# Value products two score tiles at a time at the end, a second buffer for the last normalizations, the last products in halves, and z parts marked by landing time

## The chip, the cores and the metric

The kernel runs on one core of one Trainium2 chip. The metric is device time in microseconds for one execution of the program.

## What is computed

One fused block: a layernorm, then multi-head attention and a gated MLP side by side on the same normalized input, added to the input.

```python
B, S, D, H = 1, 2048, 512, 32                 # 16 elements a head
xn = layernorm(x)
# A: attention
q, k, v = split(xn @ wqkv)                    # 32 heads
o = softmax(q @ k.T / 4) @ v
A = concat_heads(o) @ wo
# B: gated MLP, 1792 features, halves of 896
z  = gelu(xn @ w_in)
z1, z2 = z[..., :896], layernorm(z[..., 896:])
g  = einsum("ts,bsf->btf", w_sp, z2) + b_sp   # mixes the 2048 rows
Bo = (z1 * g) @ w_out
return x + A + Bo
```

All of it is float32. Most products are made of three products of high and low parts.

## The kernel before

**Attention sets the beat.** Heads go in 16 pairs `p`, queries in 4 blocks `c` of 512, keys in 16 blocks of 128, so there are N = 1024 score tiles (`order`, numbered `n`; a tile is 128 keys by 512 queries for the two heads). A tile passes three steps. `scores()` multiplies (TensorE, L1149) into one of three PSUM buffers `sl[0..2]`; `exp` turns it into a tile `pf` (ScalarE, L76; 8 buffers); `values()` multiplies a phase of CYC = 8 such tiles with V (TensorE, L1246), two tiles at a time in four column strips, summing in one `sl` buffer. Here a phase is named by its first tile: V984 takes tiles 984 to 991. The sum of the first phase of a block is copied by ScalarE, that of the second is added by VectorE (`part_out`, L1266).

**The maxima.** The softmax's maximum comes from a second pass over scores with queries on the partitions: `maxima()` (TensorE, L1163), reduced by VectorE (L868), one tile each. For 16 of them `max_fin` writes rows that go through DRAM into `qst`, as rows of the score product. The maxima run some tiles ahead of the scores and end first (n_mx == NSTEP).

**All other products** are cut into "dense slots" of two matmuls into the two banks of `dps` (L1208): Q, K, V, the MLP's two inputs, the spatial mix (`spatial`, on tiles `wsp` and parts `zs` of z2 loaded by `load_z`), the MLP's output and the attention's output (`attn_out`, 18 slots for every two row blocks). Where nothing else can go, a filler multiplies zeros (L1222).

**The order** is written out by a planner at build time: its loop takes, from the strings ORDER, one of S (score tile), M (maximum tile), D (dense slot) or V (value phase) and keeps due times `T` of each engine. What the plan says is fixed; on the chip every instruction waits on semaphores. When a generator of dense slots says "w" (`need`), the planner plans other things until the condition holds.

**The end.** The heads of group 3 (p = 12 to 14) are normalized in `norm_out`, for each `c`: loads of the sums (`os`) and of the unnormalized outputs (`ob`), a reciprocal, a trip through DRAM, products on GpSimd (L911 to L931), giving `ohl`, which `attn_out` needs for the row blocks of that `c`. One buffer `os` and one `ob` serve them all (`room["ogrp"]`). The last pair, p = 15, skips DRAM: `last_pair` (L992) spreads sums with a selector matrix, `last_norm` divides (VectorE, L998 and L1000), `last_mm` multiplies by the last rows of wo (L1007; four matmuls into two `sl` buffers), `last_add` adds to `fin` (VectorE, L1014), and SyncE stores the rows. `last_turn` decides when `last_mm` goes.

Of the kernel before, what the change touches and what calls it, by code (L numbers as in the profile page):

```python
# [47 lines left out]
CYC = 8  # L48
LOAD = 5.0
HALF = 2.7  # L50
# [8 lines left out]
def fused_block(ctx, tc, x, wqkv, wo, w_in, w_spT, b_sp, w_out, out):  # L59
# [614 lines left out]
    zp, z1s = {}, {}  # L674
# [31 lines left out]
    def spatial():  # L706
        for n, (g, (x, y)) in enumerate(units):
# [184 lines left out]
    def norm_out(g4, c):  # L892
# [31 lines left out]
        lease("ogrp", 1)  # L924
# [71 lines left out]
    def last_norm(c, acc, rec, on, k):  # L996
# [5 lines left out]
        turn.append((c, on, ends[0] + 0.1))  # L1002

    def last_mm(c, on, ks):
        for a in range(4):
            u = slice(32 * a, 32 * a + 32)
            nc.tensor.matmul(sl[ks[a // 2]][:, a % 2, :], on[u, :], sel["ones"][u, 1, :], start=True, stop=True)  # L1007
        T["P"] += 0.9
        for i, k in enumerate(ks):
            spawn(last_add(4 * c + 2 * i, k), 0, T["P"] + 0.2)  # L1010
# [23 lines left out]
    with tc.manual_schedule(engines=engines):  # L1034
# [139 lines left out]
        def has_dense(t):  # L1174
            nonlocal blocked, swap, hold, seen
            while not slots:
# [11 lines left out]
                elif it[0] == "q":  # L1188
                    hold = spent > 11 and n_pv < N
# [42 lines left out]
        def values():  # L1232
# [3 lines left out]
            window[:] = T["P"], T["P"] + CYC / 2 * ROUND  # L1236
            k = take("o")
            for n in range(n_pv, n_pv + CYC, 2):
# [3 lines left out]
                for r in range(2):  # L1242
                    pf = full.pop(n + r)
                    for j in range(2):
                        cols = VW * (2 * j + r)
                        nc.tensor.matmul(sl[k][cols:cols + VW, 0, :], vpack(kt + r, 2 * p + j), pf[:, j * 512:(j + 1) * 512], start=n == n_pv, stop=n == n_pv + CYC - 2)  # L1246
# [3 lines left out]
            n_pv += CYC  # L1250
            spawn(part_out(p, c, kt0 == 0, k), 0, T["P"] + 0.22)
# [27 lines left out]
        def last_turn(t):  # L1279
            c, on, when = turn[0]  # L1280
            if when > t or any(added.get(4 * c + 2 * i, FAR) + 0.1 > t for i in range(2)):
                return False
            if len(spare(t)) < 2:
                return False
            turn_to("L")
            ks = [take("l"), take("l")]
            last_mm(c, on, ks)
# [3 lines left out]
        while n_pv < N or queue or tasks or late or urgent or turn or slots:  # L1291
# [4 lines left out]
            if turn and (n_st - n_pv < 2 or n_pv == N) and last_turn(t):  # L1296
# [6 lines left out]
            gone = {"S": n_st == N, "M": n_mx == NSTEP, "D": ahead > 0 or not has_dense(t), "V": n_pv == N}[op]  # L1303
# [53 lines left out]
```

## Time and profile before

| | us |
|---|---|
| median of 3 runs (lowest, highest) | 1860.66 (1859.05, 1863.14) |
| the profiled execution: its own time | 1862.6 |
| the profiled execution: span of its instructions | 1860.4 |
| TensorE busy (share of the span) | 1811.4 (97%) |
| VectorE busy | 1441.5 (77%) |
| ScalarE busy | 1189.1 (64%) |
| GpSimd busy | 722.3 (39%) |
| the same, from 1765 to 1860 only: TensorE, VectorE, ScalarE | 84.8, 51.2, 49.7 of 95 |

A row of the timeline reads: start, length, engine, line, operation, output<-inputs, shapes, count, and in brackets the idle time before it and what ended that. A matmul's length includes its pipeline, so the distance between two starts is what a matmul costs. PE is TensorE, DVE VectorE, ACT ScalarE, POOL GpSimd, SP SyncE.

### The profile page before, as it was taken

To read this page: it belongs to the slowest core of one execution; us is meant where nothing else is said; L and a number is where in the kernel's file an instruction comes from. 1 tells how busy PE (TensorE), PEld (TensorE's weight loads), DVE (VectorE), ACT (ScalarE), POOL (GpSimd) and SP (SyncE) were. 2 spreads that over 40 slices of the span, in tenths; PEclk is the share of its full clock that TensorE was granted. 3 is DMA by queue.
4 is the path that set the end of the run, shared out by engine and by line. 5 is a ranking of instruction groups with operands and counts; after the bars stand their busy time and mean duration, and the time that the engine had idled before them with its cause. 6 is when DMAs were issued, how large, how long until landed. Compare 5 with 4: busy or idle time off the path is not lost.

```text
span 1860.4 us, 38081 instructions
## 1 busy us (share of the span) xinstructions
PE 1811.4 (97%) x14804; PEld 1099.5 (59%) x14804; DVE 1441.5 (77%) x1677; ACT 1189.1 (64%) x1292; POOL 722.3 (39%) x808
## 2 busy tenths in 40 slices
PE   6999999999999999999999999999999999999998
PEld 4766566655655565556565665656556566656544
DVE  6578778888887787878877787778778887887873
ACT  2157777687777777666666665666666665666655
POOL 5324342778888767222442245103422230001110
PEclk9999999999999999999999999999999999999999
DMA  6728772533565346656857558565767676575322
GB/s 227 283 98 282 277 242 87 127 92 110 136 215 134 106 113 204 156 156 162 217 166 199 157 179 206 158 150 155 193 168 182 174 185 143 129 182 149 112 78 90
DMA packets 212124, 306.14 MB, mean 165 GB/s; under 512 B 36816, under 2 KB 108048, under 8 KB 209056
## 3 DMA queue, kind: packets, MB, share of 16 engines
q1 hardware_dynamic: 202824, 273.83, 53.5%
q0 software_dynamic: 9120, 29.89, 4.8%
q8 instruction: 116, 1.90, 0.4%
q14 instruction: 64, 0.52, 0.1%
HBM read 193.80 MB, written 109.85 MB: 163 GB/s over the span
## 4 chain that ended last, share of the span: by engine, by line
PE 84%; DVE 6%; DMA 4%; POOL 3%; issue 2%; ACT 1%; SPq 1%; DVEq 0%; POOLq 0%; ACTq 0%
PE dps L1208 34%; PE sl L1246 23%; PE sl L1149 13%; PE sl L1163 12%; DVE mm L868 4%; PE dps L1222 1%; DMA zs<-z2scr 1%; DMA kscr<-qkhl 1%; SPq L132 1%; ACT pf L76 1%; POOL wsp L291 1%; DMA wsp_15r<-in_w_spT 0%; POOL wsp L289 0%; DMA wsp_0r<-in_w_spT 0%; DMA qst<-mscr 0%
## 5 line engine op out<-in xcount | busy, mean ns | idle before, releaser
L868 DVE TENSOR_REDUCE mm<-sl 128x2 f32<-128x1024 f32 x1024 | 1224.4, 1222 | 203.7 <-PE sl L1163 199.1
L76 ACT ACTIVATE pf<-sl 128x1024 f32<-128x1024 f32 x1024 | 1041.1, 1026 | 338.8 <-PE sl L1149 297.3
L1246 PE MATMUL sl<-pf,vall 128*32 128x512 f32 x4096 | 468.4, 598 | 0.7 <-DVE mm L868 0.4
L1149 PE MATMUL sl<-qst,kst 50*128 50x512 f32 x2048 | 437.8, 419 | 11.1 <-DVE mm L868 4.3
L1163 PE MATMUL sl<-kst,qst 48*128 48x512 f32 x2048 | 424.0, 406 | 4.5 <-DVE mm L868 2.2
L1208 PE MATMUL dps<-wsp,zs 64*128 64x512 f32 x2352 | 382.1, 393 | 2.6 <-DMA zs<-z2scr 2.6
L1149 PEld LDWEIGHTS sl<-qst,kst 50*128 50x128 f32 x2048 | 195.8, 184 | 218.4 <-issue 79.3
L1246 PEld LDWEIGHTS sl<-pf,vall 128*32 128x32 f32 x4096 | 120.5, 110 | 271.2 <-issue 237.4
L1163 PEld LDWEIGHTS sl<-kst,qst 48*128 48x128 f32 x2048 | 196.5, 185 | 105.9 <-ACT pf L76 55.3
L1208 PEld LDWEIGHTS dps<-wsp,zs 64*128 64x128 f32 x2352 | 229.3, 187 | 40.4 <-DMA zs<-z2scr 4.1
L76 ACT ACTIVATE e<-sl 128x512 f32<-128x512 f32 x64 | 38.3, 598 | 208.0 <-PE sl L1246 198.0
L1266 DVE TENSOR_TENSOR e<-sl,e 128x512 f32<-128x512 f32 x64 | 44.3, 692 | 136.4 <-PE sl L1246 70.2
L774 POOL TENSOR_TENSOR hhl<-z1i,hhl 128x512 fp32r<-128x512 f32 x28 | 35.9, 1292 | 275.8 <-ACT hhl L76 275.8
L1208 PE MATMUL dps<-w,xt 64*128 64x448 f32 x768 | 110.6, 368 | 1.5
L1208 PE MATMUL dps<-wout,hp 64*128 64x512 f32 x672 | 110.3, 392 | 0.0
L915 POOL TENSOR_TENSOR ob<-ob 128x512 f32<-128x512 f32 (+1 forms) x16 | 20.5, 1284 | 201.5 <-DMA ob<-rscr 186.6
L1208 PEld LDWEIGHTS dps<-w,xt 64*128 64x128 f32 x768 | 73.9, 186 | 16.0 <-issue 7.8
L1208 PEld LDWEIGHTS dps<-wout,hp 64*128 64x128 f32 x672 | 65.5, 187 | 9.1
L911 POOL TENSOR_TENSOR ob<-ob 128x512 f32<-128x512 f32 (+1 forms) x16 | 21.0, 1315 | 117.5 <-DMA ob<-escr 117.5
L441 POOL TENSOR_TENSOR qkhl<-qr,qkhl 128x512 fp32r<-128x512 f32 x24 | 30.4, 1286 | 69.9 <-ACT qkhl L76 65.8
L1208 PE MATMUL dps<-wf,zs 64*128 64x512 f32 x336 | 55.5, 392 | 0.1
L1208 PE MATMUL dps<-xnT,wqk 64*128 64x512 f32 x288 | 47.7, 395 | 1.1 <-ACT vall L76 0.4
(289 smaller groups left out, 1691.0 us busy)
## 6 DMA issues: line engine op xcount, KB each, us to landing
zs<-z2scr SPq DMA_DIRECT2D x192, 256.0 KB
escr<-e SPq DMA_DIRECT2D x60, 256.0 KB
hscr<-hhl POOLq DMA_DIRECT2D x28, 512.0 KB, 6.6
qst<-qscr SPq DMA_DIRECT2D x30, 384.0 KB
kst<-kscr SPq DMA_DIRECT2D x30, 384.0 KB
qscr<-qkhl SPq DMA_DIRECT2D x16, 512.0 KB
kscr<-qkhl SPq DMA_DIRECT2D x16, 512.0 KB
xscr<-xnT POOLq DMA_DIRECT2D x16, 512.0 KB, 5.0
```

The source lines that it names most:

```text
L76: return nc.scalar.activation(out, in_, func, **kw)
L132: nc.sync.dma_start(raw(dst), raw(src))
L441: nc.gpsimd.tensor_sub(hl[:, 1, :], raw_, hl[:, 0, :].bitcast(F32))
L774: nc.gpsimd.tensor_sub(hl[:, 1, :], z1, hl[:, 0, :].bitcast(F32))
L868: nc.vector.tensor_reduce(mmax[g][:, :, t, kc], sl[k], AX.X, ALU.max)
L911: nc.gpsimd.tensor_add(both_[rows, 0, :], both_[rows, 0, :], both_[rows, 1, :])
L915: nc.gpsimd.tensor_mul(both_[rows, 0, :], both_[rows, 0, :], both_[rows, 1, :])
L1149: nc.tensor.matmul(sl[k][:, j, :], kst[p % 2][rows, kt * P:(kt + 1) * P], qst[p % 2][rows, c * 512:(c + 1) * 512], start=True, stop=True)
L1163: nc.tensor.matmul(sl[k][:, j, :], qst[p % 2][rows, tt * P:(tt + 1) * P], kst[p % 2][rows, kc * 512:(kc + 1) * 512], start=True, stop=True)
L1208: nc.tensor.matmul(dps[:, bank, :w], lhs, rhs, start=go, stop=stop)
L1246: nc.tensor.matmul(sl[k][cols:cols + VW, 0, :], vpack(kt + r, 2 * p + j), pf[:, j * 512:(j + 1) * 512], start=n == n_pv, stop=n == n_pv + ...
L1266: nc.vector.tensor_add(e, sl[k][:, 0, :], e)
```

## The change

Four edits in one diff:

- **Phases of two.** Once all maxima are issued (n_mx == NSTEP) and at most FINE = 24 tiles are left, `values(2)` takes two tiles at a time as soon as both are ready, with scores, dense slots or fillers between. The sum of a block's eight tiles stays in one `sl` buffer (`opened`) until they are through. Nine of twelve phase starts are new.
- **Last products singly.** `last_mm` makes two matmuls into one buffer, and is queued twice.
- **A second buffer.** For g4 == 3 and odd `c`, `norm_out` takes its `ob` from the ring of 19 large pieces and leaves "ogrp" alone; `os` has two buffers. So the normalization of c = 2 need not wait for that of c = 1.
- **Parts of z.** `load_z` notes LOADZ = 5.0 after its issue as the part's landing time, and `spatial` plans other work until then. The number after which dense work is held at a stage's end goes from 11 to 8 slots.

```diff
@@ load_z, spatial
         if x == y:
             move(v, z2scr[:, x, :, 4 * i:4 * i + 4, :])
+            zland[k] = max(clock(), ends[0]) + LOADZ
             return
...
+        zland[k] = max(clock(), ends[0]) + LOADZ
...
-                yield from need(lambda: (g, s) in wsp and 4 * n + s // 4 in zp)
+                yield from need(lambda: (g, s) in wsp and zland.get(4 * n + s // 4, FAR) <= clock())
@@ norm_out
-        yield "C", lambda: room["ogrp"] > 0 and (g4 or zused[0] > OUTS)
-        lease("ogrp", -1)
-        sums = at_.tile([P, 2, 32], F32, tag="osum", name=f"os{g4}_{c}", bufs=1)
-        both_ = at_.tile([P, 2, 512], F32, tag="ogrp", name=f"ob{g4}_{c}", bufs=1)
+        own = g4 == 3 and c % 2
+        yield "C", lambda: room["big" if own else "ogrp"] > 2 * own and (g4 or zused[0] > OUTS)
+        sums = at_.tile([P, 2, 32], F32, tag="osum", name=f"os{g4}_{c}", bufs=2)
+        if own:
+            both_ = piece(f"ob{g4}_{c}").bitcast(F32)
+        else:
+            lease("ogrp", -1)
+            both_ = at_.tile([P, 2, 512], F32, tag="ogrp", name=f"ob{g4}_{c}", bufs=1)
@@ last_norm, last_mm
-        turn.append((c, on, ends[0] + 0.1))
+        for i in range(2):
+            turn.append((c, on, ends[0] + 0.1, i))
-    def last_mm(c, on, ks):
-        for a in range(4):
+    def last_mm(c, on, i, k):
+        for a in range(2 * i, 2 * i + 2):
             u = slice(32 * a, 32 * a + 32)
-            nc.tensor.matmul(sl[ks[a // 2]][:, a % 2, :], on[u, :], sel["ones"][u, 1, :], start=True, stop=True)
+            nc.tensor.matmul(sl[k][:, a % 2, :], on[u, :], sel["ones"][u, 1, :], start=True, stop=True)
@@ has_dense
-                    hold = spent > 11 and n_pv < N
+                    hold = spent > 8 and n_pv < N
@@ values
-        def values():
+        opened = []
+        def values(steps=CYC):
...
-            k = take("o")
-            for n in range(n_pv, n_pv + CYC, 2):
+            if n_pv % CYC == 0:
+                opened[:] = [take("o")]
+            k = opened[0]
+            for n in range(n_pv, n_pv + steps, 2):
...
-            n_pv += CYC
-            spawn(part_out(p, c, kt0 == 0, k), 0, T["P"] + 0.22)
+            n_pv += steps
+            if n_pv % CYC == 0:
+                opened.clear()
+                spawn(part_out(p, c, kt0 < CYC, k), 0, T["P"] + 0.22)
@@ the planner's loop
-            if turn and (n_st - n_pv < 2 or n_pv == N) and last_turn(t):
+            fine = n_mx == NSTEP and n_pv >= N - FINE
+            if turn and (n_st - n_pv < 2 or n_st == N) and last_turn(t):
                 continue
...
+            if fine and n_pv < N:
+                pair = ready.get(n_pv + 1, FAR) <= t and (opened or free)
+                if n_st < N and free and st_ok(t) and (opened or n_st - n_pv < PF) and not (pair and "s" in kind):
+                    scores()
+                    continue
+                if pair:
+                    values(2)
+                    continue
+                op, at_op = "D" if has_dense(t) else "", 0
```

Lines of the changed kernel stand a little further on: its L1157, L1171, L1216, L1230 and L1258 are L1149 (scores), L1163 (maxima), L1208 (dense), L1222 (filler) and L1246 (values) of before.

The instructions on TensorE stand as before up to the last part of z for the first unit of the spatial mix's fourth block. There, between phases V704 and V712, stood this (wsp and zs87 are the operands of the spatial mix; a dense slot is 2 matmuls):

```order
L1208 MATMUL dps_200<-wsp3_11_14528,zs86_14516 128x512 x2
L1208 MATMUL dps_200<-wsp3_12_14581,zs87_14647 128x512 x2
L1149 MATMUL sl1_202<-qst1_91,kst1_93 128x512 x2
L1208 MATMUL dps_200<-wsp3_12_14581,zs87_14647 128x512 x2
L1163 MATMUL sl2_203<-kst1_93,qst1_91 128x512 x2
L1208 MATMUL dps_200<-wsp3_12_14581,zs87_14647 128x512 x2
L1208 MATMUL dps_200<-wsp3_13_14604,zs87_14647 128x512 x4
L1149 MATMUL sl0_201<-qst1_91,kst1_93 128x512 x2
L1208 MATMUL dps_200<-wsp3_13_14604,zs87_14647 128x512 x2
L1163 MATMUL sl1_202<-kst1_93,qst1_91 128x512 x2
```

Now other work stands ahead of the first use of zs87:

```order
L1216 MATMUL dps_200<-wsp3_11_14528,zs86_14516 128x512 x2
L1230 MATMUL dps_200<-brow_85,zeror_81 128x512 x2
L1157 MATMUL sl1_202<-qst1_91,kst1_93 128x512 x2
L1171 MATMUL sl2_203<-kst1_93,qst1_91 128x512 x2
L1230 MATMUL dps_200<-brow_85,zeror_81 128x512 x2
L1157 MATMUL sl0_201<-qst1_91,kst1_93 128x512 x2
L1230 MATMUL dps_200<-brow_85,zeror_81 128x512 x2
L1171 MATMUL sl1_202<-kst1_93,qst1_91 128x512 x2
L1230 MATMUL dps_200<-brow_85,zeror_81 128x512 x2
L1157 MATMUL sl2_203<-qst1_91,kst1_93 128x512 x2
L1171 MATMUL sl0_201<-kst1_93,qst1_91 128x512 x2
L1216 MATMUL dps_200<-wsp3_12_14581,zs87_14647 128x512 x6
```

Eight of the 24 dense slots of this stretch moved behind V712, into the next three stretches (27, 27, 27 slots where 24, 24, 25 stood), and three fillers came in here.

Between V968 and V976 the attention's output for row blocks 8 and 9 needs `ohl3_2`. Before, fillers stand there; this is the start of that piece on TensorE, right behind V968:

```order
L1163 MATMUL sl0_201<-kst1_93,qst1_91 128x512 x2
L1222 MATMUL dps_200<-brow_85,zeror_81 128x512 x2
L1149 MATMUL sl1_202<-qst1_91,kst1_93 128x512 x2
L1222 MATMUL dps_200<-brow_85,zeror_81 128x512 x2
L1163 MATMUL sl2_203<-kst1_93,qst1_91 128x512 x2
L1149 MATMUL sl0_201<-qst1_91,kst1_93 128x512 x2
L1222 MATMUL dps_200<-brow_85,zeror_81 128x512 x2
L1163 MATMUL sl1_202<-kst1_93,qst1_91 128x512 x2
L1222 MATMUL dps_200<-brow_85,zeror_81 128x512 x2
```

Now dense slots stand there from the start:

```order
L1157 MATMUL sl2_203<-qst1_91,kst1_93 128x512 x2
L1171 MATMUL sl1_202<-kst1_93,qst1_91 128x512 x2
L1216 MATMUL dps_200<-wo1_18308,op8_0_19257 128x512 x4
L1157 MATMUL sl0_201<-qst1_91,kst1_93 128x512 x2
L1216 MATMUL dps_200<-wo1_18308,op8_0_19257 128x512 x2
L1216 MATMUL dps_200<-wo2_18309,op8_0_19257 128x512 x2
L1171 MATMUL sl2_203<-kst1_93,qst1_91 128x512 x2
L1216 MATMUL dps_200<-wo2_18309,op8_0_19257 128x512 x2
```

The stretches before V976, V984 and V992 held 10, 8 and 18 dense slots and the first of them 7 fillers; now each holds 18 and no filler, so that 18 dense slots fewer are left behind V992.

At the end of TensorE's program, V1000 was followed by this:

```order
L1246 MATMUL sl1_202<-pf1007_19857,vall_87 32x512 x2
L1007 MATMUL sl2_203<-sel_18215,on1_19756 128x512 x2
L1007 MATMUL sl0_201<-sel_18215,on1_19756 128x512 x2
L1149 MATMUL sl1_202<-qst1_91,kst1_93 128x512 x2
L1208 MATMUL dps_200<-wo1_18304,op14_0_19767 128x512 x6
L1208 MATMUL dps_200<-wo2_18305,op14_0_19767 128x512 x4
L1149 MATMUL sl2_203<-qst1_91,kst1_93 128x512 x2
L1149 MATMUL sl1_202<-qst1_91,kst1_93 128x512 x2
L1208 MATMUL dps_200<-wo2_18305,op14_0_19767 128x512 x2
```

Now the eight tiles of V1000 go in twos, with two score tiles and up to two dense slots between:

```order
L1216 MATMUL dps_200<-wo1_18308,op14_1_19669 128x512 x2
L1258 MATMUL sl1_202<-pf1000_19811,vall_87 32x512 x2
L1258 MATMUL sl1_202<-pf1001_19830,vall_87 32x512 x2
L1157 MATMUL sl2_203<-qst1_91,kst1_93 128x512 x2
L1216 MATMUL dps_200<-wo1_18308,op14_1_19669 128x512 x4
L1157 MATMUL sl0_201<-qst1_91,kst1_93 128x512 x2
L1258 MATMUL sl1_202<-pf1002_19845,vall_87 32x512 x2
L1258 MATMUL sl1_202<-pf1003_19851,vall_87 32x512 x2
L1157 MATMUL sl2_203<-qst1_91,kst1_93 128x512 x2
L1216 MATMUL dps_200<-wo2_18309,op14_1_19669 128x512 x4
L1157 MATMUL sl0_201<-qst1_91,kst1_93 128x512 x2
L1258 MATMUL sl1_202<-pf1004_19859,vall_87 32x512 x2
```

Tiles 1000 to 1023 are now twelve phases of two, and ahead of each stand, besides its own, one or two further score tiles (none more ahead of the last).

More of the change, by code (lines that the diff above doesn't have):

```diff
@@ L48 @@
 CYC = 8
+FINE = 24
 LOAD = 5.0
+LOADZ = 5.0
 HALF = 2.7
@@ L673, in fused_block @@
     zparts = [(g, u, i) for g, u in units for i in range(4)]
-    zp, z1s = {}, {}
+    zp, z1s, zland = {}, {}, {}
     def load_z(k):
@@ L923, in norm_out @@
         nc.gpsimd.tensor_sub(hl[rows, 1, :], both_[rows, 0, :], hl[rows, 0, :].bitcast(F32))
-        lease("ogrp", 1)
+        lease("big" if own else "ogrp", 1)
         if g4 < 3:
@@ L1245, in values @@
                         cols = VW * (2 * j + r)
-                        nc.tensor.matmul(sl[k][cols:cols + VW, 0, :], vpack(kt + r, 2 * p + j), pf[:, j * 512:(j + 1) * 512], start=n == n_pv, stop=n == n_pv + CYC - 2)
+                        nc.tensor.matmul(sl[k][cols:cols + VW, 0, :], vpack(kt + r, 2 * p + j), pf[:, j * 512:(j + 1) * 512], start=n % CYC == 0, stop=n % CYC == CYC - 2)
                 T["P"] += ROUND
@@ L1279, in last_turn @@
         def last_turn(t):
[L1280 to L1283, printed above, removed]
+            c, on, when, i = turn[0]
+            if when > t or added.get(4 * c + 2 * i, FAR) + 0.1 > t or len(spare(t)) < 2:
                 return False
             turn_to("L")
-            ks = [take("l"), take("l")]
-            last_mm(c, on, ks)
+            last_mm(c, on, i, take("l"))
             turn.pop(0)
@@ L1302, in fused_block @@
             op = "V" if n_pv == N else ORDER[line][at_op] if n_st or st_ok(t) else "M"
-            gone = {"S": n_st == N, "M": n_mx == NSTEP, "D": ahead > 0 or not has_dense(t), "V": n_pv == N}[op]
+            if fine and n_pv < N:
[7 more added lines that the diff above has]
+                op, at_op = "D" if has_dense(t) else "", 0
+            gone = {"S": n_st == N, "M": n_mx == NSTEP, "D": ahead > 0 or not has_dense(t), "V": n_pv == N}.get(op)
             if gone and n_st and n_pv < N:
```

7 lines of the change are left out of this document (3 added, 4 removed).

## The prediction

> **What bounds the kernel now.** I read the page first, then the chain of waits, then TensorE's timeline at the three places where the order of instructions changes, and VectorE's and ScalarE's beside it.
>
> ```profile
> PE 1811.4 (97%) x14804; PEld 1099.5 (59%) x14804; DVE 1441.5 (77%) x1677; ACT 1189.1 (64%) x1292; POOL 722.3 (39%) x808
> L868 DVE TENSOR_REDUCE mm<-sl 128x2 f32<-128x1024 f32 x1024 | 1224.4, 1222 | 203.7 <-PE sl L1163 199.1
> L76 ACT ACTIVATE pf<-sl 128x1024 f32<-128x1024 f32 x1024 | 1041.1, 1026 | 338.8 <-PE sl L1149 297.3
> ```
>
> TensorE is busy for 97%, so before the end a microsecond is won only where it waits or multiplies zeros. A maximum costs VectorE 1.22 us and a tile costs ScalarE 1.03. The end is another matter: there the value phases start like this.
>
> ```profile
> 1738.31 3.64 PE L1246 MATMUL sl<-pf,vall 128*32 128x512 f32 x32
> ...
> 1752.13 3.64 PE L1246 MATMUL sl<-pf,vall 128*32 128x512 f32 x32
> ...
> 1765.20 3.64 PE L1246 MATMUL sl<-pf,vall 128*32 128x512 f32 x32
> ...
> 1779.33 3.64 PE L1246 MATMUL sl<-pf,vall 128*32 128x512 f32 x32
> ...
> 1793.50 6.05 PE L1246 MATMUL sl<-pf,vall 128*32 128x512 f32 x32
> ...
> 1810.60 3.64 PE L1246 MATMUL sl<-pf,vall 128*32 128x512 f32 x32 [0.45 <-DVE mm L868]
> ...
> 1844.27 3.64 PE L1246 MATMUL sl<-pf,vall 128*32 128x512 f32 x32
> ...
> 1847.84 1.14 PE L1007 MATMUL sl<-sel,on 32*128 32x512 f32 x8
> ```
>
> These are V952, V960, V968, V976, V984, V992 and V1016 (V1000 and V1008 lie between the last two). With 9 maxima a stretch takes 13.82 us (V952 to V960), with 7 it takes 13.07. The three from V968 on take 14.13, 14.17 and 17.10, together 45.40, though they hold 9, 7 and 6 maxima. From V992 to the last phase's end (3.57 after its start, when L1007 begins) 37.24 us pass, and to the end of the span at 1860.4 another 12.56.
>
> **Prices.**
>
> ```profile
> 1292.33 0.43 PE L1163 MATMUL sl<-kst,qst 48*128 48x512 f32 x2
> 1292.69 3.64 PE L1246 MATMUL sl<-pf,vall 128*32 128x512 f32 x32
> 1296.27 0.50 PE L1149 MATMUL sl<-qst,kst 50*128 50x512 f32 x2
> ...
> 1305.62 3.64 PE L1246 MATMUL sl<-pf,vall 128*32 128x512 f32 x32
> ```
> ```profile
> 1823.12 0.13 PEld L1246 LDWEIGHTS sl<-pf,vall 128*32 128x32 f32 x4 [0.30 <-issue]
> 1823.55 0.13 PEld L1246 LDWEIGHTS sl<-pf,vall 128*32 128x32 f32 x4 [0.30 <-issue]
> ...
> 1831.38 0.86 PE L1208 MATMUL dps<-wo,op 64*128 64x512 f32 x6
> ...
> 1832.08 0.40 PE L1149 MATMUL sl<-qst,kst 50*128 50x512 f32 x2
> ```
>
> A slot costs 0.70/3 = 0.235 us. Two tiles of a value phase have two such groups of weight loads, 0.43 apart, so 0.86. Around a whole phase, maximum tile to score tile, 3.94 us pass: take off 4 x 0.86 and the maximum's slot of 0.235, and 0.27 is left for turning the array's tiling twice; the first slot after it is 0.1 late as well, so 0.36 a phase. The Trainium skill (TensorEngine Tiling (Array Packing), the constraint on mode switching) says that a change of tiling mode drains the engine, which speaks against nine more phases; it has no price, and the trace's 0.36 carries it here.
>
> **Part 1: z parts awaited (V704 to V744).**
>
> ```profile
> 1319.71 3.64 PE L1246 MATMUL sl<-pf,vall 128*32 128x512 f32 x32
> ...
> 1328.78 0.50 PE L1208 MATMUL dps<-wsp,zs 64*128 64x512 f32 x1 [0.53 <-DMA zs<-z2scr]
> 1329.73 0.49 PE L1208 MATMUL dps<-wsp,zs 64*128 64x512 f32 x1 [0.45 <-DMA zs<-z2scr]
> ...
> 1334.85 3.64 PE L1246 MATMUL sl<-pf,vall 128*32 128x512 f32 x32
> ```
>
> V704 to V712 took 15.14 us where a like stretch took 12.93 (1292.69 to 1305.62): zs87 landed late in its two halves, and behind the waiting matmul stood scores and maxima, for which ScalarE and VectorE waited in turn. Now three score and three maximum tiles and four fillers stand ahead of it. Those 10 slots are 2.35 us of TensorE, enough for the landing, but the maxima pass VectorE at 1.22 us each: from 1328.25, where the wait began, that gives 1331.9, and with three slots more 1332.6 for V712, 2.25 us sooner. The eight dense slots moved behind it are paid back: the next three stretches get 7 slots more than their dense slots and filler of before, 7 x 0.235 = 1.65. I take a gain of 0.6; the ends are a loss of 0.6 (two more fillers and a new wait of VectorE's) and a gain of 2.2 (those stretches hide the slots behind VectorE). SyncE issues zs90 to zs92 a few transfers later, with their use as much later; nothing.
>
> **Part 2: the second buffer (V968 to V992).**
>
> ```profile
> 1766.39 1.28 POOL L915 TENSOR_TENSOR ob<-ob 96x512 f32<-96x512 f32 x1 [22.01 <-DMA ob<-rscr]
> ```
> ```profile
> 1769.34 0.41 PE L1222 MATMUL dps<-brow,zeror 64*128 64x512 f32 x2
> ```
> ```profile
> 1784.11 0.96 DVE L998 RECIPROCAL on<-sl 128x128 f32<-128x128 f32 x1 [3.11 <-ACT e L76]
> ...
> 1800.65 2.36 DVE L1014 TENSOR_TENSOR fin<-sl,fin 128x1024 f32<-128x1024 f32 x2 [0.28 <-PE sl L1007]
> ```
> ```profile
> 1788.00:1790.00 2.00, 1.63 (x8) 1.00 0.00 0
> 1790.00:1792.00 2.00, 1.60 (x8) 0.89 0.00 0
> 1792.00:1794.00 2.00, 2.00 (x10) 0.50 0.00 0
> ...
> 1796.00:1798.00 2.00, 2.00 (x16) 0.50 0.23 66
> ```
>
> GpSimd gets the normalization of c = 2 to its last steps at 1766.39, after 22 us of waiting on transfers that stood behind the one buffer; TensorE fills with zeros from 1769.34. The dense work then comes late, none is left ahead of V984, and with 8 matmuls (4 slots, 0.94 us of work) in 2 us the granted clock falls to 0.50. That is why V984 took 6.05 instead of 3.64. With a buffer of its own c = 2 is ready a stretch sooner, and each stretch has its 18 dense slots.
> - V968 to V976 becomes an ordinary stretch of 9 maxima: 13.82.
> - V976 to V984: 13.07 for 7 maxima, and VectorE also has the reciprocal (0.96) and product (0.29) of the first last_norm between them: 14.3 if VectorE sets it, 13.6 if TensorE does. It took 14.17 with 8 dense slots; I take 14.2.
> - V984 to V992 was set by VectorE, as the 0.45 before V992 shows: from 1799.55 to 1810.60, 11.05 us, with two additions of 1.18 (L1014) ahead of the maxima. Now one of them comes ahead: 9.9, and the phase itself 3.57 at full clock: 13.5.
>
> Sum 41.5 against 45.4: a gain of 3.9. The ends are 2.4 (only the clock of V984 comes back) and 6.0 (TensorE sets the last two stretches: 13.6 and, for 32 slots, a phase, a turn and half a last_mm, 12.0). In SyncE's queue the loads of os and ob for c = 2 and c = 3 now stand ahead of the loads of op4 and op8; `attn_out` issues those one pair of row blocks, so one stretch, before their use, which covers them. Uncovered, the four issues would cost what they take there, a few us, and part 2 would fall to its low end.
>
> **Part 3: phases of two (V992 to the end).**
>
> ```profile
> 1826.88 0.50 PE L1149 MATMUL sl<-qst,kst 50*128 50x512 f32 x2
> ...
> 1827.51 1.03 ACT L76 ACTIVATE pf<-sl 128x1024 f32<-128x1024 f32 x1 [4.32 <-PE sl L1149]
> ...
> 1837.11 0.62 PE L992 MATMUL sl<-e,sel 128*32 128x128 f32 x16
> 1837.66 0.73 PE L1149 MATMUL sl<-qst,kst 50*128 50x512 f32 x4
> ...
> 1837.80 0.60 ACT L76 ACTIVATE e<-sl 128x512 f32<-128x512 f32 x1 [2.35 <-PE sl L992]
> ...
> 1840.45 5.61 ACT L76 ACTIVATE pf<-sl 128x1024 f32<-128x1024 f32 x6 [0.22 <-PE sl L1149]
> ...
> 1848.05 0.69 DVE L1266 TENSOR_TENSOR e<-sl,e 128x512 f32<-128x512 f32 x1 [8.34 <-PE sl L1246]
> ...
> 1853.87 2.36 DVE L1014 TENSOR_TENSOR fin<-sl,fin 128x1024 f32<-128x1024 f32 x2 [1.23 <-PE sl L1007]
> ```
>
> Maxima are over, so ScalarE's exponentials limit: 5.61/6 = 0.94 us each back to back. But with phases of eight it stood still through each: 4.32 us at V1000. Now count from V992's start, T. The phase ends at T+3.6; last_pair (0.55) and half a last_mm (0.55) take it to T+4.8; the first score tile gives an exponential 0.6 later, at T+5.5. The second reuses the same buffer, because last_pair and last_mm hold the other two, so it ends at T+8.0, and V1000 starts at about T+8.4. From there a round of two tiles costs TensorE 0.86 + 0.36 + 2 score slots 0.47 + 2 dense slots 0.47 = 2.16, and ScalarE 1.9 to 2.05; two score buffers let exponentials run under the value products. I take 2.18 a round: 11 rounds, 24.0, V1022 at T+32.4, its end at T+33.5 (0.86, turns). Against 37.24, that gains 3.8. The ends: 1 (0.25 us more a round, one late release) and 7 (24 exponentials of 0.94 and one copy of 0.60 from T+5.5 without a gap, then one round, T+30).
>
> After the last phase VectorE did 0.69, twice 1.18, 0.96, 0.29 and twice 1.18 until 1856.23, with a gap of 1.23 for the last L1007; 4.2 us of stores follow. Now one addition more falls there, but in halves the products lie under additions: about 8.0 after the phase's end instead of 8.4. A gain of 0.4.
>
> The `qst` rows for tiles from 1008 on stand behind the stores of fin2 in SyncE's queue, which wait for an addition at about T+6.5; with issue and landing that is T+11, and tile 1008 is not multiplied before T+13. Hidden by 2 us.
>
> **Sum.** 0.6 + 3.9 + 3.8 + 0.4 = 8.7. The profiled execution took 1862.6 (span 1860.4 and 2.2 around), so 1853.9 by its own time; it lies 1.94 above the median of 1860.66, and at the median's level I forecast 1852.0.
>
> **Rivals.**
> - *The small phases run one after the other* (slower). If a round's exponentials start only after its value products, it costs 1.22 for the products, 0.47 for scores, 0.6 to the first exponential and 2 x 0.94 with 0.1 to hand over: 4.3 instead of 2.18. Eleven rounds lose 23, and 1852.0 becomes 1875. It decides from 2.18 + 8.7/11 = 2.97 a round. For it: one of the three buffers is held by the open sum, and the ring has no fourth. Against it: the order has one or two further score tiles ahead of each phase, and ScalarE's six at 0.94 ran on two buffers. 0.07.
> - *The clock falls in the small phases.* In 1788 to 1792 half of TensorE's time held work and the clock halved for some 6.5 us. From V1008 on there are about 10.4 us of slots and value products in 15, 69%; no row shows which share suffices. If it falls once, about 3 us of products double: 1855.0. The Trainium skill (TensorE: Matmul & The Clock Gate, Part 1) has the clock halve after an idle window of about 3.4 us; here the records cover 3.2 of the 4 us from 1788 to 1792 and the clock fell all the same, so the rows go further than the rule. 0.12.
> - *The waits only move.* Part 1 gives nothing, part 2 only the clock, part 3 its low end: 2.4 + 1, about 1857.3, within what can be told from no change. 0.07.
> - *Everything hides.* All high ends: 2.2 + 6 + 7 + 0.4, about 1845. 0.08.
>
> **Chances.** The forecast has 0.66. A measurement of this kernel can tell about 0.2%, 3.7 us, from no change. Faster by more: 0.66 + 0.12 + 0.08 = 0.86; same 0.07; slower 0.07. The range, 1847.0 to 1857.0, leaves out the slow rival, the no-change one and part of the best: the forecast's own terms with their ends give 1847 to 1857 too.
>
> **What would show it.** Right: V984 at 3.6 us and a granted clock of 1.0 all through; no wait for zs near 1328; V968 to V992 in 40 to 43 us; starts of the small phases some 2.2 us apart, with ScalarE busy for 90% there; 12 us from the last phase to the end. Wrong: rounds of 3 us or more; a clock of 0.5 after V1008; a new wait of L1149 for `qst`; V976 to V992 no shorter than before, which would put VectorE, not the dense work, at fault.

## The result, and the profile after

The changed kernel takes 1855.80 us (median of 20 runs, 1852.68 to 1861.22) against 1861.12 of the kernel before (20 runs, 1857.67 to 1865.63): a ratio of 0.9972, interval 0.9964 to 0.9979. It is faster by 5.3 us (by the interval 3.9 to 6.7) where 8.7 were forecast. The profiled execution took 1855.84, its span 1853.9.

First the page of the changed kernel, with the busy time of the engines and the two costliest groups beside matmuls, then one row for the stretch from V968 to V992: its length, the busy time of TensorE, of its weight loads, of VectorE, ScalarE and GpSimd with their instructions, the granted clock of TensorE (1.00), the DMA engines' share and GB/s.

```profile
PE 1807.5 (97%) x14778; PEld 1093.5 (59%) x14778; DVE 1440.9 (78%) x1677; ACT 1189.6 (64%) x1292; POOL 722.0 (39%) x808
L872 DVE TENSOR_REDUCE mm<-sl 128x2 f32<-128x1024 f32 x1024 | 1223.8, 1222 | 202.2 <-PE sl L1171 195.8
L78 ACT ACTIVATE pf<-sl 128x1024 f32<-128x1024 f32 x1024 | 1041.6, 1026 | 335.1 <-PE sl L1157 298.5
```
```profile
1764.00:1806.00 42.00, 40.45 (x322) 21.73 (x324) 34.67 (x40) 24.98 (x26) 4.12 (x4) 1.00 0.30 94
```

TensorE has 26 matmuls fewer, all of them of fillers; the rest of its work is what it was, so only fillers, waits and the clock can have changed the time. The timeline of TensorE, value phases V968, V976, V984, V992, V1000, V1002 and the last one, V1022:

```profile
1763.94 3.64 PE L1258 MATMUL sl<-pf,vall 128*32 128x512 f32 x32
...
1777.74 3.64 PE L1258 MATMUL sl<-pf,vall 128*32 128x512 f32 x32
...
1792.06 3.64 PE L1258 MATMUL sl<-pf,vall 128*32 128x512 f32 x32
...
1805.56 3.64 PE L1258 MATMUL sl<-pf,vall 128*32 128x512 f32 x32
...
1814.50 1.07 PE L1258 MATMUL sl<-pf,vall 128*32 128x512 f32 x8
...
1816.64 1.06 PE L1258 MATMUL sl<-pf,vall 128*32 128x512 f32 x8
...
1839.81 1.06 PE L1258 MATMUL sl<-pf,vall 128*32 128x512 f32 x8
```

V984 takes 3.64 and no longer 6.05, and V968 to V992 13.80, 14.32 and 13.50. V992 to V1000 is 8.94, V1000 to V1022 25.31 for 11 rounds, and from 1840.87 to the end of the span 13.03. Around the parts of z, phases V704, V712, V728 and V736 start like this, and in V728's stretch stands a matmul that waits:

```profile
1317.20 3.64 PE L1258 MATMUL sl<-pf,vall 128*32 128x512 f32 x32
...
1330.12 3.64 PE L1258 MATMUL sl<-pf,vall 128*32 128x512 f32 x32
...
1358.25 3.64 PE L1258 MATMUL sl<-pf,vall 128*32 128x512 f32 x32
...
1365.14 0.50 PE L1216 MATMUL dps<-brow,onesr 64*128 64x512 f32 x2 [0.19 <-DVE z1i L756]
...
1373.84 3.64 PE L1258 MATMUL sl<-pf,vall 128*32 128x512 f32 x32
```

The 2.22 us won up to V712 (12.92 for 15.14) are paid back with 3.03 by V744; V728 to V736 alone takes 15.59 for 13.74.

The two spans differ by 6.50 us. Of these 2.51 lie ahead of V704, where the order is the same, so they are no gain: 1.26 ahead of the first phase (V0 starts at 115.96 before, at 114.70 after), and 1.61 between V600 and V608, which took 18.31 before and 16.70 after. There the granted clock of before fell to 0.50 from 1154 to 1156 us, and that of the change did not; of the ten kernels below, the three whose clock fell there took 18.17 to 18.76, the seven others 15.07 to 17.02. The rest, from the starts in the two traces:

| us | before | after | gain | forecast |
|---|---|---|---|---|
| V704 to V744 | 68.77 | 69.58 | -0.81 | +0.6 |
| V744 to V968 | 376.72 | 377.16 | -0.44 | 0 |
| V968 to V992 | 45.40 | 41.62 | +3.78 | +3.9 |
| V992 to the last phase's end | 37.31 | 35.31 | +2.00 | +3.8 |
| from there to the span's end | 12.49 | 13.03 | -0.54 | +0.4 |

V744 to V968 took 376.9 to 377.4 in the ten kernels below as well; where its 0.4 come from is open.

### The profile page after: what moved, and what is told of

Its sections match the earlier page's. It is cut to its first block, busy times and chain, and to the rows that moved or that the text cites. A ratio compares the mean times of both kernels' runs of the same rounds, so it can differ in the third digit from the quotient of the medians.

```text
span 1853.9 us, 38030 instructions
## 1 busy us (share of the span) xinstructions
PE 1807.5 (97%) x14778; PEld 1093.5 (59%) x14778; DVE 1440.9 (78%) x1677; ACT 1189.6 (64%) x1292; POOL 722.0 (39%) x808
## 4 chain that ended last, share of the span: by engine, by line
PE 87%; DVE 5%; DMA 2%; ACT 2%; issue 1%; POOL 1%; SPq 1%; DVEq 0%; ACTq 0%; POOLq 0%
PE dps L1216 35%; PE sl L1258 23%; PE sl L1157 14%; PE sl L1171 12%; DVE mm L872 3%; SPq L134 1%; PE dps L1230 1%; ACT pf L78 1%; DMA zs<-z2scr 1%; POOL wsp L293 0%; DMA wsp_11r<-in_w_spT 0%; PE sl L247 0%; PE sl L246 0%; PE sl L245 0%; PE sl L1016 0%
## 5 line engine op out<-in xcount | busy, mean ns | idle before, releaser
L1258 PE MATMUL sl<-pf,vall 128*32 128x512 f32 x4096 | 467.9, 595 | 1.0 <-DVE on L1006 0.6
L1157 PE MATMUL sl<-qst,kst 50*128 50x512 f32 x2048 | 436.0, 418 | 9.4 <-DVE mm L872 2.9
L1171 PE MATMUL sl<-kst,qst 48*128 48x512 f32 x2048 | 422.1, 405 | 4.5 <-DVE mm L872 2.4
L1216 PE MATMUL dps<-wsp,zs 64*128 64x512 f32 x2352 | 379.0, 392 | 1.6 <-DMA zs<-z2scr 1.5
L1157 PEld LDWEIGHTS sl<-qst,kst 50*128 50x128 f32 x2048 | 194.3, 184 | 221.9 <-issue 79.6
L1258 PEld LDWEIGHTS sl<-pf,vall 128*32 128x32 f32 x4096 | 119.3, 109 | 266.9 <-issue 234.3
L1171 PEld LDWEIGHTS sl<-kst,qst 48*128 48x128 f32 x2048 | 195.1, 185 | 105.0 <-ACT pf L78 52.6
L1216 PEld LDWEIGHTS dps<-wsp,zs 64*128 64x128 f32 x2352 | 226.9, 187 | 39.3 <-DMA zs<-z2scr 2.2
L1216 PE MATMUL dps<-w,xt 64*128 64x448 f32 x768 | 110.4, 368 | 1.5
L1216 PE MATMUL dps<-wout,hp 64*128 64x512 f32 x672 | 110.5, 393 | 0.0
L1216 PEld LDWEIGHTS dps<-w,xt 64*128 64x128 f32 x768 | 73.5, 186 | 16.3 <-issue 7.8
L1216 PEld LDWEIGHTS dps<-wout,hp 64*128 64x128 f32 x672 | 65.8, 187 | 9.2
L1216 PE MATMUL dps<-wf,zs 64*128 64x512 f32 x336 | 55.5, 393 | 0.1
L1216 PE MATMUL dps<-xnT,wqk 64*128 64x512 f32 x288 | 47.7, 396 | 1.1 <-ACT vall L78 0.4
```

What stands on the lines that cost most here:

```text
L1157: nc.tensor.matmul(sl[k][:, j, :], kst[p % 2][rows, kt * P:(kt + 1) * P], qst[p % 2][rows, c * 512:(c + 1) * 512], start=True, stop=True)
L1171: nc.tensor.matmul(sl[k][:, j, :], qst[p % 2][rows, tt * P:(tt + 1) * P], kst[p % 2][rows, kc * 512:(kc + 1) * 512], start=True, stop=True)
L1216: nc.tensor.matmul(dps[:, bank, :w], lhs, rhs, start=go, stop=stop)
```

## The experiments

What part of the change does what, and why the end gained 1.5 and not 4.2, was tried with ten kernels. The stretches below are from starts in one profiled execution of each; "V992-end" reaches to the end of the span, "rounds" is V1000 to V1022, and "tail" goes from the end of the last phase to the end of the span.

| kernel | ratio to before (interval) | V704-V744 | V968-V992 | V992-end | rounds | tail |
|---|---|---|---|---|---|---|
| before | 1 | 68.77 | 45.40 | 49.80 | - | 12.49 |
| the change | 0.9972 (0.9964-0.9979) | 69.58 | 41.62 | 48.34 | 25.31 | 13.03 |
| only_z | 0.9992 (0.9982-1.0002) | 69.57 | 46.08 | 49.38 | - | 12.44 |
| only_own | 0.9977 (0.9967-0.9987) | 68.85 | 42.79 | 49.33 | - | 12.44 |
| whole | 0.9972 (0.9961-0.9982) | 69.57 | 42.82 | 49.00 | 25.19 | 13.57 |
| no_fine | 0.9990 (0.9981-0.9999) | 69.63 | 41.58 | 51.71 | - | 12.79 |
| lp_closed | 0.9962 (0.9950-0.9974) | 69.59 | 41.56 | 47.66 | 24.44 | 13.24 |
| lpc_noz | 0.9964 (0.9952-0.9976) | 68.81 | 41.59 | 47.44 | 24.42 | 13.02 |
| copy_dve | 0.9976 (0.9967-0.9985) | 69.65 | 41.58 | 48.39 | 25.56 | 12.84 |
| dps_turn | 0.9979 (0.9968-0.9990) | 68.86 | 42.96 | 51.63 | 31.94 | 10.58 |
| lp_dps | 0.9966 (0.9951-0.9980) | 68.90 | 41.57 | 47.34 | 23.81 | 13.53 |
| one_h | 0.9977 (0.9965-0.9989) | 68.86 | 41.56 | 47.80 | 26.93 | 10.62 |

**only_z: the parts of z alone.** `FINE = 0`, no buffer of its own (`own = 0`; `os` keeps two), whole turns of `last_mm`, which the plan now costs at 1.1 (before 0.9).

> Only the parts of z awaited; the rest as before. Theory A (what is put off is paid back, and more, because the evacuation of a finished unit of the spatial mix no longer lies under a value phase): V704 to V712 about 2.2 us shorter, V712 to V744 about 3 us longer, the whole 0 to 0.8 us slower, ratio 1.0000 to 1.0005. The prediction's theory: 0.6 us faster, the three stretches behind longer by 1.65 only.

V704 to V744 took 69.57, and it takes 69.57 to 69.65 in all six kernels that wait for the parts and 68.77 to 68.90 in the six that do not. So this part loses 0.8 us, though the whole kernel's time cannot show it. The evacuation of a finished unit shows where (VectorE, `z1i` from `dps`, before and in the change):

```profile
1361.49 1.28 DVE L752 SCALAR_TENSOR_TENSOR z1i<-dps,z1i 128x512 f32<-128x512 f32 x2
```
```profile
1363.81 1.28 DVE L756 SCALAR_TENSOR_TENSOR z1i<-dps,z1i 128x512 f32<-128x512 f32 x2
```

Before, it ran beside the products of V728, which start at 1361.77. In the change V728 starts at 1358.25 and is through when the evacuation begins, and the dense work behind it waits until 1365.14. The sizes fit: V712 to V720 and V720 to V728 hold two and three slots more and cost 0.49 and 0.72 more, as slots would; V728 to V736 holds two more and costs 1.85. No run moves the evacuation alone.

**only_own: the second buffer alone.** `FINE = 0`, whole turns (costed at 1.1), `need(... in zp)` and 11 slots as before.

> Only the second buffer for the last normalizations; z parts, whole last turns and phases of eight as before. Theory A (the stretches are set by VectorE once dense work is there, and the clock stays up): V968 to V992 takes 41.6 us instead of 45.4, V984 3.6, and the end behind V992 stays at 49.8 although 18 dense slots are gone from it, because ScalarE sets it: 3.8 us less in all, ratio about 0.998. Theory B (only the clock of V984 comes back): 43.0 and 2.4 us less. Theory C (the dense work taken forward shortens the end too, 18 slots of 0.235): 8 us less.

V992, V1000 and the last `last_mm`:

```profile
1806.77 3.64 PE L1258 MATMUL sl<-pf,vall 128*32 128x512 f32 x32 [0.44 <-DVE mm L872]
...
1818.02 3.64 PE L1258 MATMUL sl<-pf,vall 128*32 128x512 f32 x32 [0.47 <-ACT pf L78]
...
1843.59 1.14 PE L1015 MATMUL sl<-sel,on 32*128 32x512 f32 x8
```

V968 to V992 is 42.79: the buffer alone gives 2.6 of the 3.8. Of these 2.4 are V984, which takes 3.64 again for 6.05, so theory B's 43.0 is nearer than theory A's 41.6. VectorE still holds V992 (the 0.44), since both additions of the whole turn stand ahead of the maxima. From V992 on nothing is won by the 18 dense slots that are no longer there: V1000 waits for ScalarE (`pf`), and the end takes 49.33, against 49.38 in only_z, which still has them. Theory C is out.

**whole: the change with whole turns.**

```diff
-        for i in range(2):
-            turn.append((c, on, ends[0] + 0.1, i))
+        turn.append((c, on, ends[0] + 0.1))
...
-    def last_mm(c, on, i, k):
-        for a in range(2 * i, 2 * i + 2):
+    def last_mm(c, on, ks):
+        for a in range(4):
```

> The change with last_mm whole again (four matmuls into two buffers, costed at 1.1 in the plan). Theory A (four matmuls in four row groups run side by side and take 1.1 us, and two take as long): V992 to V1000 takes 8.4 instead of 8.9 since no half stands there, but V984 to V992 gets a second addition and takes 14.7 instead of 13.5; from the end of V1022 to the end of the span 12.6 instead of 13.1. In all within 1 us of the change. Theory B (halves cost half): V992 to V1000 8.9 less 0.55 too, but the end is no shorter and the whole is 1 us or more slower than the change.

First the busy time of the engines and the granted clock by stretches of 2 us, then V984's `last_mm` and V992 on the timeline:

```profile
1806.00:1808.00 2.00, 1.44 (x8) 0.56 (x6) 2.00 (x2) 1.59 (x3) 0.00 (x0) 1.00 0.00 0
1808.00:1810.00 2.00, 1.70 (x8) 0.40 (x12) 1.80 (x7) 1.60 (x2) 0.00 (x0) 0.54 0.04 10
```
```profile
1797.16 1.14 PE L1015 MATMUL sl<-sel,on 32*128 32x512 f32 x8
...
1808.30 5.24 PE L1258 MATMUL sl<-pf,vall 128*32 128x512 f32 x32 [0.44 <-DVE mm L872]
```

V984 to V992 takes 14.70, 1.2 more than in the change, as theory A said, and here the clock fell to 0.54 as V992 began, so that its products take 5.24 us for 3.64. In only_own the same stretch of 14.71 ran at full clock, so the fall is not certain. The whole kernel's ratio is the change's, 0.9972. And eight matmuls take 1.14, in the change four take 1.13. In two places theory A missed: V992 to V1000 took 9.19 for 8.4, of which the clock's 1.6 are a part, and the tail took 13.57 for 12.6. Without the fall V992 to the end would be 47.4, an estimate from these rows (49.00 less 1.6), and the halves would be worth 1.2 in V984 to V992 and cost 0.9 behind it.

**no_fine: the change without the small phases.** `FINE = 24` becomes 0.

> The change with the value phases left at eight tiles to the end (parts of z, the second buffer and the single halves of last_mm stay). It isolates the small phases. Theory A (the small phases gain little, because the three events in them that the prediction had not priced, last_pair in the open sum's buffer, the copy of the finished sum, and halves of last_mm that take as long as whole ones, eat what they win): V968 to V992 in 41.6 us as in the changed kernel; from V992 to the span's end 49.3, as measured with the second buffer alone, against 48.3 in the changed kernel, so about 1 us more in all, 1856.8. Theory B (the prediction's sum: phases of two gain 3.8): V992 to the end about 52, so 1859.6. Theory C (the small phases cost more than they win): below 48 from V992, 1855 or less.

V992, V1000, the last phase, and the `last_mm` behind it:

```profile
1806.89 3.64 PE L1258 MATMUL sl<-pf,vall 128*32 128x512 f32 x32
...
1819.17 3.64 PE L1258 MATMUL sl<-pf,vall 128*32 128x512 f32 x32 [0.47 <-ACT pf L78]
...
1842.17 3.64 PE L1258 MATMUL sl<-pf,vall 128*32 128x512 f32 x32 [0.19 <-ACT pf L78]
...
1845.74 1.13 PE L1016 MATMUL sl<-sel,on 32*128 32x512 f32 x4
```

Theory B is right: the end takes 51.71, so the small phases are worth 3.4 us. That is near the forecast 3.8, but not against before: halves in phases of eight take 2.4 more than whole turns there (51.71 to 49.33), 1.0 of it between V992 and V1000 and 1.5 between V1008 and V1016, in each of which a half of 1.13 stands where only_own has none; V1000 to V1008, with one half for one whole turn, gives 0.5 back, and the tail costs 0.4. The two edits meet as 3.4 - 2.4.

**lp_closed: `last_pair` kept out of an open sum.**

```diff
-            while sel and urgent and urgent[0][2] <= T["P"]:
+            while sel and urgent and urgent[0][2] <= T["P"] and not opened:
```

> The change, but last_pair waits until the open sum of the value products is through, so that no division reads a buffer that value products are still writing. Theory A (the value products of V1010 waited for the reciprocal, and the product of the division for V1010, because both lie in one PSUM buffer): the rounds from V1008 to V1012, 2.58 and 3.10, become 2.0 to 2.2; the pair then costs one round behind V1014 instead, 0.5 to 1 us; 0.5 to 1 us less in all. Theory B (rounds are long because TensorE turns its tiling): they stay at 2.6 and 3.1, no gain.

In the change, `last_pair` of the third row block goes into the buffer in which the sum from V1008 on is still open; its reader holds up V1010, and V1010 holds up its second reader. Where the last turn goes, and what a finished sum costs at V1016, stands below it (timeline of the change: TensorE, VectorE, ScalarE):

```profile
1809.57 1.13 PE L1016 MATMUL sl<-sel,on 32*128 32x512 f32 x4
...
1825.40 1.06 PE L1258 MATMUL sl<-pf,vall 128*32 128x512 f32 x8 [0.65 <-DVE on L1006]
1826.53 0.29 DVE L1008 TENSOR_TENSOR on<-sl,on 128x128 f32<-128x128 f32 x1 [1.19 <-PE sl L1258]
...
1831.93 0.60 ACT L78 ACTIVATE e<-sl 128x512 f32<-128x512 f32 x1
...
1834.77 0.19 PEld L1157 LDWEIGHTS sl<-qst,kst 50*128 50x128 f32 x2 [0.45 <-ACT pf L78]
1835.20 1.06 PE L1258 MATMUL sl<-pf,vall 128*32 128x512 f32 x8
...
1838.76 1.13 PE L1016 MATMUL sl<-sel,on 32*128 32x512 f32 x4
```

With the pair moved, the two rounds from V1008 to V1012 fall from 2.58 and 3.10 to 1.89 and 2.13, 1.66 less. Of this 0.63 comes back at V1016 to V1018 (3.73 for 3.10), where the pair now stands in the finished sum's buffer:

```profile
1830.56 0.96 DVE L1006 RECIPROCAL on<-sl 128x128 f32<-128x128 f32 x1 [4.49 <-PE sl L1000]
...
1831.55 0.60 ACT L78 ACTIVATE e<-sl 128x512 f32<-128x512 f32 x1 [0.92 <-DVE on L1006]
...
1832.18 0.29 DVE L1008 TENSOR_TENSOR on<-sl,on 128x128 f32<-128x128 f32 x1 [0.67 <-ACT e L78]
```

Three readers of one buffer go one after the other, and only then may a score tile have it. In the code the sum takes the first 512 columns of the buffer (`sl[k][:, 0, :]`) and the pair the second 512 (`sl[k][:, 1, :]`); the rows show an order kept over the buffer as a whole. (The Trainium skill, PSUM — Partial Sum Buffer, the section on bank collisions, says that two engines may not access the same bank and partitions at once, reads included. No run here shows whether that asks for an order between the two parts of the buffer, or whether a finer one would do.) The end, V992 to the span's end, became 0.7 shorter, as theory A said.

**lpc_noz: lp_closed without the parts of z.**

> The change, with last_pair kept out of the buffer of an open sum, and with the parts of z no longer awaited (the order around V704 as before). Theory A (awaiting the parts of z loses 0.8 us between V704 and V744, as counted with it alone): V704 to V712 15.1 again and V704 to V744 68.8 instead of 69.6; the time 0.8 below that of the same kernel with the parts awaited, 1855.1. Theory B (it gains 0.6, as predicted): 1856.5. Locally the two are told apart by the starts of V704 and V744; by the time hardly.

V704 to V744 is 68.81 and theory A holds there. The time, 0.9964, cannot be told from lp_closed's 0.9962.

**copy_dve: lp_closed with the last finished sum copied by VectorE.**

```diff
+            if opens and p == NP - 1 and c == 3:
+                e = parts[p, c] = at_.tile(...)
+                yield "D", td(512)
+                nc.vector.tensor_copy(e, sl[k][:, 0, :])
```

> The change, with last_pair kept out of the buffer of an open sum, and the copy of the last finished sum of a block (e15_3) made by VectorE, which has no maxima left, instead of ScalarE. Theory A (the long rounds from V1016 to V1020, 3.73 and 1.77 with last_pair moved, come from that copy: 0.60 on ScalarE ahead of the exponentials, and the buffer is held by it): the round from V1016 to V1018 falls to about 2.6, V1000 to V1022 from 24.4 to about 23.5, and the time by 0.9 to 1855.0. Theory B (ScalarE is not short there; the block change costs what it does because the buffer stays taken until any engine has copied it, and VectorE's copy is no shorter): the round stays within 0.3 of 3.7 and the time at 1855.9.

```profile
1839.16 1.13 PE L1016 MATMUL sl<-sel,on 32*128 32x512 f32 x4
...
1840.41 1.22 DVE L1022 TENSOR_TENSOR fin<-sl,fin 128x1024 f32<-128x1024 f32 x1 [1.09 <-PE sl L1016]
...
1841.69 0.49 PE L1157 MATMUL sl<-qst,kst 50*128 50x512 f32 x2 [0.26 <-DVE fin L1022]
```

The round became 4.85, longer than either theory said. The edit also moved a turn: one half of `last_mm` now stands in this round, and the score tile behind it waits for that half's addition. So it does not tell what the copy costs; it shows that a half between small phases holds a score buffer for its product and its addition, 2.5 us.

**lp_dps: the pair in the dense buffer.** lpc_noz, and once dense work is over `last_pair` writes into `dps`.

> The change without the parts of z and with the last_pair of the third row block, which follows the phase at V1014, written into the dense work's buffer (idle there but for fillers) instead of the finished sum's. All else is as in the version that keeps last_pair out of an open sum. Theory A (the block change is long because the finished sum's buffer is read by one engine after the other: reciprocal 0.96, copy 0.60, product 0.29, and the score tile that needs this buffer waits for all three): now the copy is all that the buffer waits for; the round from V1016 to V1018 falls from 3.72 to 2.5 to 2.9, V1000 to V1022 from 24.4 to about 23.5, and the time by 0.9 against that version. Theory B (what costs is ScalarE's 0.60 for the copy and the order of score tiles and fillers around it): the round stays at 3.4 to 3.8 and the time where it was.

The copy and the reciprocal now run side by side, and the score tile behind V1016 no longer waits for the pair's readers (it starts 1.00 after V1016, where lpc_noz has 1.67):

```profile
1829.84 0.60 ACT L78 ACTIVATE e<-sl 128x512 f32<-128x512 f32 x1
1829.89 0.96 DVE L1007 RECIPROCAL on<-dps 128x128 f32<-128x128 f32 x1 [4.49 <-PE dps L1001]
...
1833.29 1.06 PE L1265 MATMUL sl<-pf,vall 128*32 128x512 f32 x8
```

The round is 3.11 (from 3.72). Theory A is right in kind and gave up to twice too much: 0.6 of the 1.8 above a plain round in lpc_noz were the readers in a row. What makes up the other 1.2 no run shows; the copy's 0.60 on ScalarE may be a part. The tail was 0.5 longer here (13.53) with the same products and additions, and that is the clock: it fell at 1846, where the last half of `last_mm` took 1.67 us for 1.13.

```profile
1844.00:1846.00 2.00, 1.83 (x8) 0.79 (x10) 1.90 (x3) 0.00 (x0) 0.00 (x0) 1.00 0.73 277
1846.00:1848.00 2.00, 2.00 (x8) 0.64 (x6) 1.20 (x2) 0.00 (x0) 0.00 (x0) 0.53 0.96 359
```

**dps_turn: the late halves in the dense buffer.** lpc_noz with the copy on VectorE, a half costed 1.07, and from V1016 on `last_pair` and the halves of `last_mm` also in `dps`, as soon as they can.

> A version meant to beat both: the change without the parts of z, the copy of e15_3 on VectorE, and the last_pair and late halves of last_mm in the dense work's buffer as soon as no dense work is left, so that the three score buffers stay with the score tiles and the halves of the second and third row block's normalization go between the small phases instead of behind the last. Theory A (a buffer held and turns postponed until every score tile is out are what part 3 and the tail lost): V1000 to V1022 stays at 23.5 to 25, and behind the last phase only two halves are left instead of four, so the tail falls from 13.0 to about 11.5; the time to 1853.5. Theory B (each half costs TensorE 1.1 wherever it stands, and the rounds are set by TensorE): what leaves the tail comes back in the rounds, V1000 to V1022 at 26 to 27, and the time stays at 1855 to 1856.

A half that waits for the one before it, then the stretches of 2 us behind it:

```profile
1833.77 1.13 PE L1024 MATMUL dps<-sel,on 32*128 32x512 f32 x4 [0.88 <-DVE fin L1030]
```
```profile
1832.00:1834.00 2.00, 1.12 (x12) 0.42 (x6) 1.51 (x2) 1.02 (x1) 0.00 (x0) 1.00 0.00 0
1834.00:1836.00 2.00, 2.00 (x12) 0.41 (x12) 1.90 (x2) 0.56 (x2) 0.00 (x0) 0.89 0.72 268
1836.00:1838.00 2.00, 2.00 (x12) 0.55 (x6) 0.17 (x1) 0.56 (x2) 0.00 (x0) 0.50 1.03 383
```

The tail fell to 10.58, below the 11.5 expected. But three halves between V1016 and V1018 left TensorE waiting, no filler could go into the taken `dps`, and the clock fell to 0.50 for ten microseconds: V1000 to V1022 took 31.94, more than either theory said. This is the prediction's rival of the clock, in a kernel with longer waits than the change has. The price of 1.07 also put both halves of the first turn ahead of V992 (V984 to V992 14.84), and V992 to V1000, now without a half, took 7.55 for 8.94.

**one_h: one half a round.** lpc_noz with the late halves in `dps`, at most one between two phases.

> The change without the parts of z, last_pair kept out of an open sum, and once no dense work is left each half of last_mm goes into the dense work's buffer, one half a round, so that the halves of the second and third row block stand between the small phases from V1012 to V1022 and only the last block's two halves stay behind the last phase. Earlier, three such halves came in a burst between two phases, and the granted clock fell to 0.50 there. Theory A (a half costs TensorE 1.1 to 1.3 wherever it stands, turns included): the tail falls from 13.0 to about 10.6, and V1000 to V1022 rises from 24.4 to about 27; the time stays within 0.5 of the version without it. Theory B (a half hides under the two exponentials of its round): V1000 to V1022 at about 25 and the time 1.9 less. Theory C (the clock falls again without fillers): a granted clock of 0.5 for 6 us somewhere after V1012, and V1000 to V1022 at 30.

```profile
1826.05 1.13 PE L1024 MATMUL dps<-sel,on 32*128 32x512 f32 x4
...
1833.37 1.13 PE L1024 MATMUL dps<-sel,on 32*128 32x512 f32 x4
...
1843.89 0.70 PE L1024 MATMUL dps<-sel,on 32*128 32x512 f32 x2 [0.34 <-DVE on L1009]
1843.90 0.70 PE L1024 MATMUL sl<-sel,on 32*128 32x512 f32 x2
```

Theory A, by its numbers: the tail is 10.62, the rounds 26.93, and V992 to the end takes 47.80, 0.4 more than in lpc_noz. What leaves the tail comes back between the phases, 0.8 us a half. The profiled execution took 1853.4, but the median is 1858.13. The mean granted clock of each execution says a little more: it was 0.997 to 0.999 in the five shortest (1852.04 to 1855.56) and 0.994 to 0.996 in the three longest (1859.72 to 1860.71). So in the long ones the clock stood low for longer; where, no trace shows. The last two rows show the other side: two halves of different row strips into two buffers start 0.01 apart.

The best versions are lp_closed, lpc_noz and lp_dps (0.9962, 0.9964, 0.9966); their intervals overlap each other and the change's 0.9972. By starts, lpc_noz is 1.7 us ahead of the change: 0.8 at V704 to V744, 0.9 from V992 to the end.

## Why the prediction was right, and where it was off

**Part 1 (+0.6, measured -0.8).** The wait went as said and V712 came 2.22 sooner (2.25). The step that failed is the payback: 7 slots at 0.235 made 1.65, and it was 3.03. Five of the seven cost 1.21 in the first two stretches, as priced. V728 to V736 cost 1.85 for the other two: moving the dense slots also moved the end of the spatial unit, whose evacuation no longer lay under a value phase and made the dense work behind it wait. That this is the reason is read from the rows and not tried by itself. The low end of the part, -0.6, was exceeded by 0.2.

**Part 2 (+3.9, measured +3.8).** 13.82, 14.2 and 13.5 were forecast, 13.80, 14.32 and 13.50 measured. The clock stayed at 1.00 and V984 at 3.64, which alone is 2.4. only_own shows that 1.2 of the gain is not the buffer's but the single halves': one addition instead of two ahead of the maxima. The prediction had counted that (11.05 to 9.9).

**Part 3 (+3.8, measured +2.0).** The rival of phases that run one after the other is out: seven plain rounds took 1.77 to 2.15, 1.97 on average, below the forecast 2.18. ScalarE was busy for 86% and 84%:

```profile
1815.00:1825.00 10.00, 9.75 (x88) 3.81 (x80) 1.31 (x2) 8.61 (x10) 0.00 (x0) 1.00 0.01 2
1825.00:1835.00 10.00, 8.82 (x62) 3.19 (x62) 1.86 (x3) 8.38 (x10) 0.00 (x0) 1.00 0.00 0
```

What was mis-sized are the other four of the eleven, 11.5 us where four at 2.18 make 8.7: two at V1008 to V1012 (`last_pair` in the open buffer; lp_closed takes 1.66 from them), the last, with a half (2.72; without one, in one_h, 1.66), and V1016 to V1018 (3.10), where the finished sum is copied. lp_dps has 3.11 there with nothing but the sum in the buffer, so readers in a row are not the reason in the change; what is, no run shows. All three were in the order of instructions and were not priced. That plain rounds were priced 0.2 too dear was luck: it covers 1.5 of the 2.8 that the four cost beyond 2.18. The other term is "half a last_mm 0.55". It took 1.13, as much as a whole one, once on the way to V1000 (8.94 where 8.4 was forecast; 7.55 without it, in dps_turn) and once ahead of V1022. The rival of the clock did not come true in the change's trace; of the eight kernels with small phases, one traced execution each, only dps_turn shows a fall between V1000 and V1022. No wait for `qst` appeared.

**Tail (+0.4, measured -0.5).** The step that failed is "one addition more". With small phases the turns wait until every score tile is out, so both halves for the rows of c = 1, whose normalization ended at 1812.57, are added only now; in no_fine they stand behind V1000 and V1008. Start, length and idle time of VectorE's first addition, the adjoining halves, and the last addition of the change:

```profile
1840.00 1.23 DVE L1022 TENSOR_TENSOR fin<-sl,fin 128x1024 f32<-128x1024 f32 x1 [11.38 <-PE sl L1016]
...
1841.24 1.17 PE L1016 MATMUL sl<-sel,on 32*128 32x512 f32 x8
...
1848.75 1.23 DVE L1022 TENSOR_TENSOR fin<-sl,fin 128x1024 f32<-128x1024 f32 x1 [0.26 <-PE sl L1016]
```

VectorE stood for 11.38 us and then had six additions to make, where before it made four behind the last phase. The halves are not at fault: `whole`, with the same six and whole turns, has a longer tail (13.57), so there they save 0.5. dps_turn and one_h show that the tail can lose 2.4, and that the rounds then pay.

**The sum.** 3.8 + 2.0 - 0.8 - 0.5 is 4.5 by the traces, 0.4 less with V744 to V968; the medians give 5.3. Both lie inside the range, near its upper end, as the three terms that fell short all fell to one side. Two sums of the prediction are slightly off, without effect on this: 37.24 less 33.5 is 3.7 and not 3.8, and the ends of its terms add up to 1845 and 1857.5, not to 1847 and 1857.

## What to carry to other kernels

Work that is moved takes its evacuation with it: ask under which phase the last step of each moved piece lies, not only how many slots it has. A sum that stays open in a buffer must have that buffer for itself, because the sum and the readers of another result in it wait for each other (V1010 for the reciprocal, the product for V1010). And before a matmul is halved, see along which dimension: half of the row strips is not half of the time.

## What the hardware showed

- Two of four row strips took 1.13 us (4 records), all four 1.14 (8 records), and two halves in a row 1.17: the strips run side by side, so half of them saves nothing. The Trainium skill (TensorE: Matmul & The Clock Gate, Part 3) says that what packing gains is concurrency of the strips; the rows agree. By that rule and the 1.14 of a whole turn the estimate for a half would have been 1.1 and not 0.55.
- The granted clock fell to about half in whole from 1808, behind 2 us with 1.44 of matmul records, in dps_turn from 1835, behind 2 us with 1.12, and in lp_dps at 1846, behind 4 us with 3.52. It kept 1.00 through 2 us with 1.35 in only_own (1805 to 1807), with 1.29 in the change (1827 to 1829) and with 1.05 in one_h (1830 to 1832). So the records of the 2 us ahead do not decide by themselves; what does was not settled.
